# Loading two token tiles by transposing DMA in place of TensorE transposes, with the first loads redistributed over two issuing queues

## The chip, the cores and the metric

One NeuronCore of a Trainium2 chip runs the whole program. The metric is the device time of one execution in microseconds (us). The kernel before took 288.73 us in the median of three runs (288.58 to 288.88). The profile below comes from one further execution of 288.21 us, whose span from first to last instruction is 287.0 us.

## The reference

The input is x, 2048 tokens of 640 values (bf16). Two branches are computed from it and mixed by a gate per token:

```python
x = A_x
g = _sigmoid((x * gate_w).sum(-1, keepdims=True))
a = _A_ref(x, A_wqkv, A_w_phi, A_wo)              # linear attention, 32 heads of 20
b = _B_ref(x, B_w_gate, B_w_up, B_w_down)         # SwiGLU, 1728 hidden columns
return g * a + (1 - g) * b
```

In the attention branch q, k and v are projections of x. q and k go through w_phi (20x20 for each head), and the softmax of the result and of its negative, side by side, are the features. The k features and v are summed over all tokens to a small matrix for each head, the q features multiply it, and the result goes through wo.

## The kernel before, in words

The tokens are cut into 16 tiles of 128 (t0 to t15), and four tiles make a block of 512. TensorE needs x with its 640 columns on the partitions, so each token tile lives in SBUF as `xT[:, t, c, :]`, five 128x128 pieces. There are two ways in which a tile gets there:

- Tiles 0 to 3 are loaded as they lie into `xs` (`load_x`, L369, on the queue that `XQ` at L361 names), transposed on TensorE by five matmuls against the identity into PSUM (`xpose`, L458, recorded at L308), and copied to `xT` by VectorE (recorded at L320).
- Tiles 4 to 15 are read by transposing DMAs on SyncE's queue straight into `xT` (`load_xt`, L372, recorded at L349).

The q and k weights are premultiplied by w_phi on chip: `load_wt` (L391) reads five row blocks of the k weights by transposing DMAs into `wT`, `w_blocks` (step Y, L559) spreads `wph` into `wbd` on VectorE and GpSimd, and `premult` (steps M0 to M4, L565) multiplies them.

Every instruction goes through a small recorder (`_Tracker.run`, L145), which keeps the order of the program for each engine and adds the semaphore waits that the data needs. The order is written out by hand in two lists. `LOADS` (L33) is issued first: x0 is the plain load of tile 0, w0 to w4 are the five row blocks of the v weights (160 KB each, queue by `WQ`, L362), g the gate vector, f0 the first 256 gate and up columns, h is w_phi, k0 to k4 are the `wT` transposing DMAs, t4 to t15 those of the token tiles. SyncE's and ScalarE's issues follow that list, each in its own order. `ORDER` (L38) is the computation: H is warm-up matmuls, X a tile's transposes, `U t.c` the c-th fifth of the v projection of tile t (two matmuls, `vpart`, L499), V a whole v projection (ten matmuls), F0.k the k-th 128 gate and up columns for block 0 (five matmuls on `wg`, five on `wu`), K, S, P, E the steps of the k features.

At the start ORDER is H0 to H12, X0, G, X1, then the v projections of tiles 0, 1 and 2 interleaved by weight row block, with X2 and X3 put between them, then V3, Y, F0.1, M1, M0 and so on.

Two groups of waits on a semaphore value that has long been reached stand in the code: `NPEW` (L20) waits in TensorE's stream in `kv_end` (step N, L749), after the k features are summed, and `NWAIT` (L19) in ScalarE's in `fitem`. They wait for nothing.

`load_phi` (L387) makes ScalarE wait for the landing of w3 before it issues the w_phi load. ScalarE's table load and its first copies out of PSUM stand behind that in its stream.

Of the kernel before, what the change touches and what calls it, by code (L numbers as in the profile page):

```python
# [6 lines left out]
P = 128  # L7
# [9 lines left out]
NV = 6  # L17
NWARM = 2
NWAIT = 6  # L19
NPEW = 24  # L20
FP = 120 * NCH
FK = FP + 8
ACTF = mybir.ActivationFunctionType
# [7 lines left out]


LOADS = """  # L33
x0 w0 x1 g w1 x2 w2 x3 w3 w4 f0 h k0 k1 t4 k2 k3 k4 t5 t6 t7 t8 t9 t10 t11 t12 t13 t14 t15 q0 q1 q2 q3
q4 f1 f2
"""

ORDER = """  # L38
H0 H1 H2 H3 H4 H5 H6 H7 H8 H9 H10 H11 H12 X0 G X1 U0.0 U1.0 U0.1 X2 U1.1 U2.0 U0.2 U1.2 U2.1
X3 U2.2 U0.3 U1.3 U2.3 U0.4 U1.4 U2.4 V3 Y F0.1 M1 i3 M0 F0.0 M2 V4 M3 M4 K0 K1 I S0 V6 V5 S1 P0  # L40
K3 K2 P1 E0 V9 K4 E1 S3 V7 P3 K5 S2 V8 V10 S4 P2 P4 E2 R0 E3 K6 S5 P5 S6 i4 E4 V14 K7 K8 P6 V15 S7
R2 E5 K9 S8 P7 R1 E6 K10 S9 V12 P8 E7 P9 K11 S10 P10 F0.2 R3 F1.2 E8 E9 K12 E10 S11 S12 K14 S14
V11 K13 P11 P12 E11 K15 P14 R4 S13 P13 F1.9 S15 P15 E12 V13 T F1.8 E13 F1.11 E14 Q1 E15 Q0 Q2 N A0
# [10 lines left out]
class _Tracker:  # L54
# [90 lines left out]
    def run(self, eng, fn, reads=(), writes=(), dma=False):  # L145
        rkeys = list(dict.fromkeys(k for a in reads for k in self.keys_of(a)))
        wkeys = list(dict.fromkeys(k for a in writes for k in self.keys_of(a)))
        need = {}

        def req(ev, raw):  # L150
            if ev is None:
                return
            s, v = ev
            if s == eng and not dma and (eng == "pe" or not raw):
                return
            if v > need.get(s, 0):
                need[s] = v

        for k in rkeys:
            for kk in self._conflicts(k):  # L160
                req(self.lastw[kk], True)
                if k[0] == "psum":
                    for s, v in self.readers[kk].items():
                        req((s, v), False)
        for k in wkeys:
            for kk in self._conflicts(k):
                req(self.lastw[kk], True)
                for s, v in self.readers[kk].items():
                    req((s, v), False)
        self._wait(eng, need)  # L170
        ins = fn()
        if dma:
            sn = "d%d" % self.ndma
            self.ndma += 1
            self._add_sem(sn)
            inc = 16
        else:
            sn, inc = eng, 1
        ins.then_inc(self.sem[sn], inc)
        self.cnt[sn] += inc  # L180
        v = self.cnt[sn]
        snap = dict(self.known[eng])
        if not dma:
            snap[sn] = max(snap.get(sn, 0), v)
        self.evknow.setdefault(sn, {})[v] = snap
        ev = (sn, v)
        for k in wkeys:
            self.lastw[k] = ev
            self.readers[k] = {}
        for k in rkeys:  # L190
            r = self.readers[k]
            if r.get(sn, 0) < v:
                r[sn] = v
        return ev


def _build(nc, A_x, A_wqkv, A_w_phi, A_wo, B_x, B_w_gate, B_w_up, B_w_down, gate_w, out):
    tr = _Tracker(nc)
    pe, act, dve, pool, sp = nc.tensor, nc.scalar, nc.vector, nc.gpsimd, nc.sync
# [3 lines left out]
    def sb(name, shape, dtype):  # L203
        t = nc.alloc_sbuf_tensor(name, list(shape), dtype)
        tr.reg(t, "sbuf", nc.lookup_mloc(t).addr)
        return t
# [6 lines left out]
    wg = sb("wg", [P, 5, F_FFN], BF16)  # L213
    wu = sb("wu", [P, 5, F_FFN], BF16)
# [61 lines left out]
    def bank(b, c0, c1, r0=0, r1=P):  # L276
        return ps[r0:r1, b * 512 + c0:b * 512 + c1]
# [38 lines left out]
    def copy(e, o, i):  # L316
        if e == "act":
            return actop(o, i, ACTF.Copy)
        eo = tr.eng[e]
        return run(e, lambda: eo.tensor_copy(o, i), [i], [o])  # L320

    def tt(e, o, a, b, op):
        eo = tr.eng[e]
        return run(e, lambda: eo.tensor_tensor(o, a, b, op), [a, b], [o])  # L324
# [9 lines left out]
    def reduce(o, i):  # L334
        return run("dve", lambda: dve.tensor_reduce(o, i, AX.X, ALU.add), [i], [o])  # L335
# [8 lines left out]
    def dma(e, dst, src, transpose=False):  # L344
        eo = tr.eng[e]

        def fn():
            if transpose:
                return eo.dma_start_transpose(dst, src)  # L349
            return eo.dma_start(dst, src)  # L350
        rd = [src] if src.tensor.name in tr.base else []
        wr = [dst] if dst.tensor.name in tr.base else []
        return run(e, fn, rd, wr, dma=True)
# [5 lines left out]


    XQ = ["sp", "act", "act", "act"]  # L361
    WQ = ["act", "sp", "sp", "sp", "act"]  # L362
    x2 = A_x[0]
    out2 = out[0]

    def load_rows(e, dst, c, c0):
        return dma(e, dst, A_wqkv[c * P:(c + 1) * P, c0:c0 + D])
# [5 lines left out]
        dma("sp", xT[:, t, :, :], x2[t * P:(t + 1) * P, :], transpose=True)  # L373

    def load_ffn(c0, c1):
        dma("sp", wg[:, :, c0:c1], B_w_gate[:, c0:c1].rearrange("(c p) j -> p c j", p=P))
        dma("sp", wu[:, :, c0:c1], B_w_up[:, c0:c1].rearrange("(c p) j -> p c j", p=P))

    wv_evs = []

    def load_wv(c):
        wv_evs.append(load_rows(WQ[c], wvg[:, c, 0:D], c, 2 * D))

# [1 line left out]
        dma("sp", gwr[0:5, :], bass.AP(gate_w.tensor, gate_w.offset, [[P, 5], [1, P]]))  # L385

    def load_phi():  # L387
        tr._wait("act", dict([wv_evs[3]]))
        dma("act", wph[:, :, :], A_w_phi.rearrange("h e f -> (h e) f").rearrange("(c p) f -> p c f", p=P))

    def load_wt(which, m):  # L391
# [9 lines left out]
    H0 = [0, 6, 12, 19, 25]  # L401
    H1 = [7, 13, 20, 26, 32]
# [172 lines left out]
    def kv_finish():  # L575
        for bk, j0, j1 in ((KV0, 0, 8), (KV0 + 1, 8, NCH)):
            n = j1 - j0
            i = bank(bk, 0, 63 * n, 0, 120).rearrange("p (j h d) -> p j h d", h=3, d=DH + 1)
            tt("dve", zt[0:120, j0:j1, :], i[:, :, :, DH],
               hmask[0:120, :].unsqueeze(1).to_broadcast([120, n, 3]), ALU.mult)  # L580
        reduce(zf[0:120, :], zt[0:120, :, :])
        copy("dve", zh[0:120, 0:NCH], zf[0:120, :])
        for bk, j0, j1 in ((KV0, 0, 8), (KV0 + 1, 8, NCH)):
            n = j1 - j0
            i = bank(bk, 0, 63 * n, 0, 120).rearrange("p (j h d) -> p j h d", h=3, d=DH + 1)
            for hh in range(3):
                tt("dve", kvsb[0:120, j0:j1, 20 * hh:20 * hh + 20], i[:, :, hh, 0:DH],
                   hmask[0:120, hh:hh + 1].unsqueeze(1).to_broadcast([120, n, DH]), ALU.mult)
# [160 lines left out]
    def kv_end():  # L749
        for _ in range(NPEW):  # L750
            pe.wait_ge(tr.sem["pe"], 1)
        kv_finish()
        ring["n"] = 4

    ops = {
        "H": lambda i: warm(), "i": fills, "X": xpose, "G": gcol, "U": vpart, "V": vtile,
        "M": lambda m: premult(1, m), "R": lambda m: premult(0, m),
        "K": ktile, "S": knorm, "P": kmul, "p": lambda t: kmul(t, "dve"), "E": kvtile, "x": load_x, "t": load_xt, "w": load_wv, "g": load_gate, "h": load_phi, "k": lambda m: load_wt(1, m), "q": lambda m: load_wt(0, m),
        "f": lambda i: load_ffn(FCUT[i], FCUT[i + 1]), "L": load_late_weights, "T": tail_weights, "J": gates,
        "Y": w_blocks, "I": kv_begin, "N": kv_end, "Z": z_row,  # L760
        "Q": qtile, "A": qsum, "B": qden, "C": qscale, "c": qmul,
        "F": fitem, "O": oitem, "D": ditem,
# [6 lines left out]
def bass_gated_mix__linear_kernel_hedgehog__swiglu_ffn__prompt_kernel(  # L769
    nc: bass.Bass,  # L770
    A_x: bass.AP,
    A_wqkv: bass.AP,
    A_w_phi: bass.AP,
    A_wo: bass.AP,
    B_x: bass.AP,
    B_w_gate: bass.AP,
    B_w_up: bass.AP,
    B_w_down: bass.AP,
    gate_w: bass.AP,
    out: bass.AP,  # L780
):
    _build(nc, A_x, A_wqkv, A_w_phi, A_wo, B_x, B_w_gate, B_w_up, B_w_down, gate_w, out)
# [28 lines left out]
```

The softmax here doesn't subtract the row's maximum and nothing guards it: scores larger than these inputs give would overflow.

## Time and profile before

| what | value | where it is from |
|---|---|---|
| median of three runs | 288.73 us | the times |
| span of the profiled execution | 287.0 us | the page |
| TensorE busy | 284.1 us, 1979 matmuls | the page, part 1 |
| granted TensorE clock | 1.0 | the cores' list |
| matmuls on `xs` (the transposes) | 20, from 3.8 to 7.8 us | the answer on the tile `xs` |
| first matmul of F0.1 | 11.19 us | the timeline |
| hardware queue of SyncE (q1) | 47400 packets, 20.43 MB | the page, part 3 |
| hardware queue of ScalarE (q10) | 1520 packets, 0.87 MB | the page, part 3 |

Times on the timeline count from the start of the span. A row of the timeline gives start, length, engine, source line (that of the recording helper), operation, the tiles written and read, and how many instructions were merged into the row; "SPq" and "ACTq" are DMA issues on SyncE and ScalarE. The landing of a DMA is given as the time from its issue. A matmul's length on the page covers its whole passage through the array; successive ones overlap, and what counts is the distance between their starts.

### The profile page before, as it was taken

The numbers are of one execution on the slowest core, as the hardware profiler recorded it, in microseconds if no ns is written. First come the engines' busy times: TensorE is split into PE (matmuls) and PEld (weight loads), VectorE is DVE, ScalarE is ACT, GpSimd is POOL, SyncE is SP. The second block draws the span as 40 slices with busy tenths as digits, with TensorE's granted clock in tenths as the row PEclk, the third lists the DMA queues.
The fourth block names the chain that finished last, engine by engine and source line by source line (L and its number), as shares of the span: only waits on it lengthen the run. The fifth ranks groups of instructions, "written<-read, shape, count | busy, mean of one in ns | idle before, by whom it ended". The sixth has DMA issues, their size and how long they took to land.

```text
span 287.0 us, 4972 instructions
## 1 busy us (share of the span) xinstructions
PE 284.1 (99%) x1979; PEld 174.5 (61%) x1979; DVE 163.3 (57%) x243; ACT 152.4 (53%) x256; POOL 159.8 (56%) x125
## 2 busy tenths in 40 slices
PE   8999999999999999999999999999999999999997
PEld 6667777575644545557775556675554446666776
DVE  2337748576569978689991465970317899100000
ACT  0767778576775465683535753225676552234112
POOL 8286999879446789836543438350754558501000
PEclk9999999999999999999999999999999999999999
DMA  7977697000010598202383002061020006210101
GB/s 234 192 113 127 113 279 279 3 1 2 0 50 0 123 290 162 50 2 50 66 157 69 6 1 50 2 149 43 2 50 0 3 1 123 53 46 0 49 23 48
DMA packets 48944, 21.62 MB, mean 75 GB/s; under 512 B 39384, under 2 KB 48792, under 8 KB 48920
## 3 DMA queue, kind: packets, MB, share of 16 engines
q1 hardware_dynamic: 47400, 20.43, 31.5%
q10 hardware_dynamic: 1520, 0.87, 1.0%
q8 instruction: 16, 0.26, 0.4%
q14 instruction: 8, 0.07, 0.1%
HBM read 9.29 MB, written 2.62 MB: 42 GB/s over the span
## 4 chain that ended last, share of the span: by engine, by line
PE 99%; DVE 0%; issue 0%
PE ps L296 97%; PE ps L478 1%; PE ps L308 0%; DVE xT L320 0%; DVE osb L737 0%; DVE wvg L320 0%
## 5 line engine op out<-in xcount | busy, mean ns | idle before, releaser
L324 POOL TENSOR_TENSOR hT<-hT,us 128x512 bf16<-128x512 bf16 (+1 forms) x56 | 65.0, 1174 | 65.1 <-DVE hT L328 47.5
L328 DVE SCALAR_TENSOR_TENSOR hT<-hT,ps 128x512 bf16<-128x512 bf16 (+1 forms) x56 | 37.4, 683 | 66.8 <-ACT hT L314 53.0
L296 PE MATMUL ps<-xT,wg 128*128 128x512 bf16 x260 | 64.6, 379 | 0.0
L296 PE MATMUL ps<-xT,wu 128*128 128x512 bf16 x260 | 64.6, 379 | 0.0
L296 PE MATMUL ps<-wd,hT 128*128 128x320 bf16 (+2 forms) x462 | 63.9, 295 | 0.0
L324 POOL TENSOR_TENSOR ph<-eq,qc 128x1320 bf16<-128x1320 bf16 x16 | 42.4, 2647 | 25.6 <-DVE qc L638 20.8
L296 PEld LDWEIGHTS ps<-wd,hT 128*128 128x128 bf16 x462 | 44.5, 98 | 17.5 <-issue 0.2
L296 PE MATMUL ps<-wqk,xT 128*128 128x320 bf16 x320 | 47.7, 299 | 0.0
L314 ACT ACTIVATE hT<-ps 128x512 bf16<-128x512 f32 (+2 forms) x64 | 36.4, 569 | 16.8 <-PE ps L296 16.5
L296 PEld LDWEIGHTS ps<-xT,wu 128*128 128x128 bf16 x260 | 25.5, 98 | 30.6
L314 ACT ACTIVATE us<-ps 128x512 bf16<-128x512 f32 (+1 forms) x56 | 33.5, 598 | 18.5 <-PE ps L296 17.3
L314 ACT ACTIVATE osb<-ps,omg 128x640 bf16<-128x640 f32 (+2 forms) x17 | 12.9, 758 | 55.4 <-PE ps L296 55.4
L296 PEld LDWEIGHTS ps<-xT,wg 128*128 128x128 bf16 x260 | 25.1, 98 | 27.8 <-ACT osb L314 0.8
L324 POOL TENSOR_TENSOR ekr<-ekr,krec 128x1280 bf16<-128x1280 bf16 x16 | 37.4, 2358 | 5.8 <-DVE krec L338 5.8
L296 PEld LDWEIGHTS ps<-wqk,xT 128*128 128x128 bf16 x320 | 30.5, 98 | 13.1 <-issue 0.4
L314 ACT ACTIVATE eq<-ps 128x640 bf16<-128x640 f32 x32 | 22.4, 704 | 20.9 <-POOL ph L324 10.8
L335 DVE TENSOR_REDUCE ksum<-ekr 128x64 f32<-128x1280 bf16 x16 | 23.5, 1471 | 11.7 <-ACT ekr L314 11.7
L314 ACT ACTIVATE ekr<-ps 128x640 bf16<-128x640 f32 x32 | 22.3, 704 | 8.7 <-PE ps L296 8.2
L335 DVE TENSOR_REDUCE qz<-eq 128x64 f32<-128x1280 bf16 x16 | 23.6, 1478 | 2.6 <-ACT eq L314 2.6
L296 PE MATMUL ps<-wog,oT 128*128 128x320 bf16 (+2 forms) x165 | 24.7, 294 | 0.0
L296 PE MATMUL ps<-wvg,xT 128*128 128x320 bf16 (+1 forms) x160 | 24.1, 299 | 0.1
L335 DVE TENSOR_REDUCE qw<-ez 128x64 f32<-128x1280 bf16 x16 | 23.6, 1477 | 0.0
(73 smaller groups left out, 188.6 us busy)
## 6 DMA issues: line engine op xcount, KB each, us to landing
out_dram<-osb SPq DMA_DIRECT2D x15, 160.0 KB, 2.0
wd<-in_B_w_down_dram SPq DMA_DIRECT2D x1, 2080.0 KB, 9.2
wg<-in_B_w_gate_dram SPq DMA_DIRECT2D x1, 1040.0 KB, 10.0
wu<-in_B_w_up_dram SPq DMA_DIRECT2D x1, 1040.0 KB, 12.2
wg<-in_B_w_gate_dram SPq DMA_DIRECT2D x1, 800.0 KB, 6.1
wu<-in_B_w_up_dram SPq DMA_DIRECT2D x1, 800.0 KB, 7.7
wog<-in_A_wo_dram SPq DMA_DIRECT2D x2, 375.0 KB, 7.1
xs<-in_A_x_dram ACTq DMA_DIRECT2D x3, 160.0 KB, 4.2
```

The lines of the kernel that those rows point to most:

```text
L296: last = pe.matmul(o, lhsT=l, rhs=r, start=st, stop=sp_, skip_group_check=sk)
L314: return run("act", lambda: act.activation(o, i, func, scale=scale), rd, [o])
L324: return run(e, lambda: eo.tensor_tensor(o, a, b, op), [a, b], [o])
L328: return run("dve", lambda: dve.scalar_tensor_tensor(out=o, in0=a, scalar=s, in1=b, op0=op0, op1=op1), rd, [o])
L335: return run("dve", lambda: dve.tensor_reduce(o, i, AX.X, ALU.add), [i], [o])
L478: last = pe.matmul(bank(2 * pr, 0, P), lhsT=c, rhs=c, start=True, stop=True)
```

## The change

Tiles 2 and 3 are no longer loaded into `xs` and transposed on TensorE. They come as `t2` and `t3`, transposing DMAs on SyncE's queue, directly behind w1. The v weight rows w2 and w3, the first gate and up columns (f0, two DMAs) go from SyncE's queue to ScalarE's. The w_phi load loses its wait for w3. ORDER loses X2 and X3; the v projections of tiles 0 and 1 stay interleaved by fifths, and that of tile 2 becomes a whole step, V2, ahead of V3. TensorE's group of empty waits at step N grows from 24 to 44, and SyncE gets four at the same place. On TensorE ten matmuls go, on VectorE three copies.

```diff
-NPEW = 24
+NPEW = 44
 LOADS = """
-x0 w0 x1 g w1 x2 w2 x3 w3 w4 f0 h k0 k1 t4 k2 k3 k4 t5 t6 ...
+x0 w0 x1 g w1 t2 t3 w2 w3 w4 f0 h k0 k1 t4 k2 k3 k4 t5 t6 ...
 ORDER = """
-H0 ... H12 X0 G X1 U0.0 U1.0 U0.1 X2 U1.1 U2.0 U0.2 U1.2 U2.1
-X3 U2.2 U0.3 U1.3 U2.3 U0.4 U1.4 U2.4 V3 Y F0.1 M1 i3 M0 F0.0 M2 V4 M3 M4 K0 ...
+H0 ... H12 X0 G X1 U0.0 U1.0 U0.1
+U1.1 U0.2 U1.2 U0.3 U1.3 U0.4 U1.4 V2 V3 Y F0.1 M1 i3 M0 F0.0 M2 V4 M3 M4 K0 ...
-    WQ = ["act", "sp", "sp", "sp", "act"]
+    WQ = ["act", "sp", "act", "act", "act"]
     def load_ffn(c0, c1):
-        dma("sp", wg[:, :, c0:c1], ...)
-        dma("sp", wu[:, :, c0:c1], ...)
+        e = "act" if c0 == 0 else "sp"
+        dma(e, wg[:, :, c0:c1], ...)
+        dma(e, wu[:, :, c0:c1], ...)
     def load_phi():
-        tr._wait("act", dict([wv_evs[3]]))
         dma("act", wph[:, :, :], ...)
     def kv_end():
         for _ in range(NPEW):
             pe.wait_ge(tr.sem["pe"], 1)
+        for _ in range(4):
+            sp.wait_ge(tr.sem["pe"], 1)
```

## The prediction, made before the changed kernel ran

> **What bounds the kernel now.** I read the page's busy shares and its chain by engine first:
>
> ```profile
> PE 284.1 (99%) x1979; PEld 174.5 (61%) x1979; DVE 163.3 (57%) x243; ACT 152.4 (53%) x256; POOL 159.8 (56%) x125
> ...
> PE 99%; DVE 0%; issue 0%
> ```
>
> TensorE is busy for 284.1 of 287.0 us and the chain that ends last runs through it alone. Busy does not mean dense, so next the chain in order of time (start, length, what):
>
> ```profile
> 3.77 0.72 PE ps L308 x5
> 4.50 0.02 issue
> 4.52 0.42 DVE xT L320
> 4.94 0.10 DVE wvg L320
> 5.04 0.05 issue
> 5.09 1.00 PE ps L296 x6
> 6.08 0.32 PE ps L308 x5
> 6.40 1.37 PE ps L296 x10
> 7.78 0.28 PE ps L308 x5
> 8.05 69.40 PE ps L296 x640
> ```
>
> Until 5.09 the chain waits for data and copies. From 5.09 on it is TensorE without a break; the starts in the timeline confirm it (the 24 v matmuls from 7.89 to 11.19 stand 137.5 ns apart). So whatever leaves TensorE's stream after 5.09 comes off the end one for one, and whatever makes it stop is added one for one. The two rows with L308 after 5.09 are X2 and X3. Last, the DMA issues in the timeline, and the answers on the tiles `wT` and `xT` (duration of an issue min/median/max in ns, then time to landing in us):
>
> ```profile
> 2.69 0.45 ACTq L350 DMA_DIRECT2D wvg<-in_A_wqkv_dram  x1
> 3.00 0.43 SPq L350 DMA_DIRECT2D wg<-in_B_w_gate_dram  x1
> 3.48 0.53 SPq L350 DMA_DIRECT2D wu<-in_B_w_up_dram  x1
> 4.05 4.23 SPq L349 DMA_TRANSPOSE wT<-in_A_wqkv_dram  x2
> 7.30 0.40 ACTq L350 DMA_DIRECT2D wph<-in_A_w_phi_dram  x1
> ```
>
> ```profile
> L349 SPq DMA_TRANSPOSE wT<-in_A_wqkv_dram x5: 1277/1299/2820, 4.0 to 12.3; - x5
> DMA to landing us min/median/max: 3.8/4.7/6.2
> ```
>
> ```profile
> L349 SPq DMA_TRANSPOSE xT<-in_A_x_dram x12: 1277/1278/2122, 8.3 to 27.7; - x12
> DMA to landing us min/median/max: 2.9/3.9/4.9
> ```
>
> A transposing DMA holds SyncE for 1.28 us against 0.4 for a plain one. The first of all (L349, at 4.05) held it 2.82.
>
> **What the Trainium skill says.** "TensorE: Matmul & The Clock Gate", section "Wait — 56ns, not 53.3ns?", gives 55.6 ns between warm matmuls of 128 columns; here the transposes of X3 start 56 ns apart, five in 0.28 us. "DMA: Bandwidth & Descriptors", section "Issuing engines are not separate DMA queues", says that SyncE's and ScalarE's DMAs share the same 16 engines. The trace agrees: w1, x2, w2, x3, w3, w4, from both queues, landed at 5.47, 5.91, 6.34, 7.05, 7.29, 7.79, one 160 KB tile in 0.46 us. So moving loads between queues buys no bandwidth, only order and issue time. Section "Queues, rings and completion order" of that page says that a DMA engine takes turns between the queues by packet. Between 5.0 and 5.5 the packet records show 65 packets of SyncE's queue and 67 of ScalarE's, which fits.
>
> **TensorE's part.** Between the first U matmul (5.09) and F0.1 (11.19) lie 6.10 us. The 40 v matmuls there, 30 in U steps and 10 in V3, take 40 x 137.5 ns = 5.50. The remaining 0.60 is X2 (5.95 to 6.24), X3 (7.61 to 7.89) and a 0.03 wait for x2. After the change 20 matmuls are U steps and 20 are V2 and V3: the same 40. Best case **-0.60 us**. VectorE's three copies (0.65 and 0.49 us of its time) hide under TensorE; nothing waits for VectorE there afterwards, so they count nothing.
>
> **The deadlines this sets.** With TensorE never stopping, the data is needed at: w2 after 8 matmuls, 6.19; w3 6.74; w4 7.29; t2 7.84; t3 9.21; wg 10.59; wu 11.67; M1 (wT1 and `wbd`) 12.75, which was 13.35.
>
> **The supply.** *ScalarE's queue.* w2 takes the slot of x2 (issued 1.73, landed 5.91), in time. w3 and w4 come in the slots at 2.21 and 2.69, whose loads landed at 7.05 and 7.79. But two plain tiles have left SyncE's queue ahead of them, 2 x 0.46, replaced by transposed packets that cannot start until their issue is over (3.4) and w1's are out (4.60). I take w3 6.2, w4 6.8; both bounds (6.1 to 7.0, 6.4 to 7.6) reach at most 0.3 past the deadline. wg and wu are issued 0.2 later than before and landed at 8.72 and 9.75; there is 1.9 us to spare.
> *t2.* Issued at 2.06. Lower bound: the median 3.9 gives 6.0. A transposed tile has 640 packets of 256 B (18 ns each on one of 16 engines) against 55 ns for the 1280 B packets of a weight row and 27 for those of wg. Taking turns from 4.60 on, 40 turns per engine, some 18 with rows (73 ns) and 22 with wg (45 ns), end at 6.9; w1 landed 0.87 after its last packet, so 7.8. With the 2.82 us issue: 8.5. Deadline 7.84.
> *t3.* Issued at 3.4. Lower bound 7.3. Forty turns with wg behind t2: 8.7, landed 9.6. With the long first issue 10.4. Deadline 9.21.
> Which value I take: for w_phi, issued on ScalarE at 7.30 while SyncE generated transposes, the first packet came 2.8 us later (x0: 1.0). If wg is held likewise it starts at 6.0, not 5.0, and t2 lands near 7.2, t3 near 9.0. The 2.82 I put down to wg and wu queued ahead (1280 small packets): the wu issue at 38.08, behind three such loads, also took 1.24 in place of 0.5. That queue is empty at 2.06. So I take both **in time, 0**.
> *The later transposes.* t2 and t3 (2 x 1.32 with the gap between issues) stand where w2, w3, wg, wu took 1.99 (2.06 to 4.05), so wT0 and all behind move by +0.65, or by -0.9 if the 1.54 extra goes with wg and wu. wT4 has 1.1 to spare (landed 17.04, used 18.14), t6 1.35, later tiles more. With -0.60 for TensorE at worst 0.15 late; I take 0.
> *w_phi.* Issued at 4.2 instead of 7.30, but behind wg and wu. Y needs 1.58 from landing (11.38) to the last `wbd` (12.96), so it must land by 11.2. Bounds: 8.3 (its 4.1 from issue) and 11.6 (after wu at 10.5, its 640 packets in turns with transposes 1.2). Taken 10.5: 0; at worst +0.4. ScalarE's table load was free to run at 7.79 and is now at 5 to 7, ahead of the first copy (9.46); nothing behind it is delayed.
>
> **The empty waits.** In TensorE's records 24 of them are 11 instructions, 109 ns apart, from 74.87 to 75.96. The wait for VectorE that follows was over at 76.16, and the next matmul started at 77.29: the array had 17 matmuls in stock. Ten more instructions are 1.09 us and bring that wait to about 77.15, the matmul to 77.25 to 77.4. Cost 0 to 0.1; taken **+0.03**. Behind them stands the whole remaining stream. SyncE's one more wait instruction falls between 39.3 and 79.1, where it issues nothing: 0.
>
> **Sum.** 287.0 - 0.60 + 0.03 = 286.43 of span. The median run (288.73) lies 1.73 above this span, so **288.2 us**.
>
> **Rivals.**
> 1. *Late by a little.* The queues take strict turns, t3 lands at 9.4 to 10.3 and V3 waits: F0.1 starts at t3 + 1.42, 10.8 to 11.7 against 11.19. For: the packet counts above. Against: w_phi's long start. 288.4 to 289.2, middle 288.8.
> 2. *Slower.* The first transposing DMA costs 2.82 by itself, wherever it stands; t2 lands at 8.5, t3 at 10.4, F0.1 starts at 11.8, 0.6 later than before: 289.4. It decides as soon as t3 lands after 9.77. With `wbd` late as well, up to 290. For: the 2.82 is on record and is the first. Against: the backlog explains it too, and a queue backlog is seen again at 38.08.
> 3. *The empty waits eat the gain.* If the stock of matmuls were smaller by ten then they would cost up to 0.6: 288.7. Against: the 17 counted.
>
> **Chances.** In time 0.50 (own range 288.0 to 288.4), rival 1 with rival 3 0.20, rival 2 0.30. A measurement here can tell about 0.2%, 0.58 us: the full gain is just that, so I split the first case in halves: faster 0.25, same 0.25 + 0.20 = 0.45, slower 0.30. Range 288.0 to 289.9: it leaves out the worst of rival 2 and the best of case one, under 2 in 10.
>
> **What would show it.** Right: no L308 rows after 5.09; v matmuls 137.5 ns apart from 5.09 on; F0.1 at 10.59; t2 landed before 7.84, t3 before 9.21, its issue 1.3 us; the matmul after step N without a gap. Wrong: TensorE idle before V2, V3 or M1 with a DMA or `wbd` as what ended it, a first issue of 2.8, a hole of tenths after the waits at step N. A move of over 0.7 us either way with F0.1 at 10.6 would mean that something after the start counts that I have taken as rigid.

## The result and the profile after

The changed kernel took **290.14 us** in the median of four runs (289.86 to 290.28), the kernel before, now in four runs, 288.81 (288.58 to 289.17). The ratio is 1.0044 with a 95% interval of 1.0026 to 1.0061: slower by 0.4%, and above the range of the prediction. The profiled execution was one of 289.86 us with a span of 288.6, against 288.21 and 287.0 before: +1.6.

The page of the changed kernel, first its busy times, then its chain by engine:

```profile
PE 284.3 (99%) x1969; PEld 174.5 (60%) x1969; DVE 162.3 (56%) x240; ACT 152.6 (53%) x256; POOL 159.8 (55%) x125
...
PE 95%; DMA 3%; SPq 1%; issue 0%; DVE 0%
```

TensorE has its ten matmuls less, and its share of the chain has gone from 99% to 95%: a DMA has come in. The chain in order of time (start, length, what) names it:

```profile
2.07 1.32 SPq L349
3.39 0.05 issue
3.43 7.98 DMA xT<-in_A_x_dram
11.41 0.05 issue
11.46 67.65 PE ps L296 x626
```

One transposing DMA, t3, issued at 3.43, lands 7.98 us later at 11.41. TensorE starts again at 11.46. In the timeline of the same kernel (the bracket gives the idle time ahead of a row and what ended it):

```profile
4.91 5.00 PE L296 MATMUL ps<-wvg,xT 128*128 128x320 bf16 x30
...
11.46 1.55 PE L296 MATMUL ps<-wvg,xT 128*128 128x320 bf16 x10 [1.54 <-DMA xT<-in_A_x_dram]
...
12.84 1.24 PE L296 MATMUL ps<-xT,wg 128*128 128x512 bf16 x5
```

The 30 matmuls of U and V2 run through; V3 stands 1.54 us for t3; F0.1 starts at 12.84 in place of 11.19. That is +1.65, the whole difference of the spans: from F0.1 to the end it is 275.8 us in both kernels. Behind F0.1 there is no other loss. The answer on the tile `xT` (issue in ns min/median/max, then landing in us) shows how far t3 lies off:

```profile
L349 SPq DMA_TRANSPOSE xT<-in_A_x_dram x14: 1272/1278/2552, 2.1 to 29.1; - x14
DMA to landing us min/median/max: 2.9/3.3/8.0
```

The rest of what was to be watched: the first transposing issue took 1.32, t2 landed at 7.58, w2, w3 and w4 at 5.67, 6.28 and 7.22, wg, wu and w_phi at 9.18, 11.30 and 11.93. At step N, the last matmuls ahead of the empty waits and the first one behind them, before:

```profile
74.58 2.88 PE L296 MATMUL ps<-wqk,xT 128*128 128x320 bf16 x20
...
77.29 0.22 PE L308 MATMUL ps<-ident,zh 120*128 120x120 bf16 x1
```

and after:

```profile
76.23 2.88 PE L296 MATMUL ps<-wqk,xT 128*128 128x320 bf16 x20
...
78.94 0.22 PE L308 MATMUL ps<-ident,zh 120*128 120x120 bf16 x1
```

2.71 us from start to start in both: twenty more waits cost nothing.

What the 16 DMA engines did meanwhile is in the table by stage (each row a stretch in us, its length, the busy shares and counts of the five engines, the granted clock, the DMA share, and last the GB/s). Before:

```profile
5.00:6.00 1.00, 0.91 (x7) 0.56 (x8) 0.47 (x3) 0.00 (x0) 0.94 (x2) 1.00 1.03 358
6.00:7.00 1.00, 1.00 (x12) 0.72 (x12) 0.65 (x2) 0.00 (x0) 1.00 (x3) 1.00 1.08 363
7.00:8.00 1.00, 1.00 (x12) 0.79 (x11) 0.00 (x0) 0.21 (x1) 0.17 (x1) 1.00 1.16 335
8.00:9.00 1.00, 1.00 (x10) 0.69 (x8) 0.49 (x1) 1.00 (x1) 0.00 (x0) 1.00 1.59 268
```

After:

```profile
5.00:6.00 1.00, 1.00 (x6) 0.52 (x6) 0.42 (x1) 0.97 (x1) 0.94 (x2) 1.00 1.17 224
6.00:7.00 1.00, 1.00 (x7) 0.66 (x6) 0.00 (x0) 0.31 (x1) 1.00 (x3) 1.00 1.18 242
7.00:8.00 1.00, 1.00 (x10) 0.71 (x8) 0.00 (x0) 0.00 (x0) 0.16 (x1) 1.00 1.16 257
8.00:9.00 1.00, 1.00 (x9) 0.73 (x8) 0.00 (x0) 0.69 (x3) 0.00 (x0) 1.00 1.26 239
```

The DMA share adds up packet times that overlap, so it passes 1; it is much the same in both. But in these four us the engines bring 962 KB instead of 1324 (the sums of the last column). The packet records have longer packets in the mean: 1280 B took 55 to 58 ns before (5 to 7 us) and 95 between 5 and 6 us after; 512 B took 27 or 28 before (6 to 8 us) and 37 to 52 after (6 to 10 us). The typical packet is as it was: the median of the 1280 B ones stays at 55, and 24 of the 137, of up to 614 ns, make the mean. (Fewer bytes and dearer 1280 B packets turn up again below in kernels where t3 is in time, so they don't set the changed kernel apart.) The records also show a stop. t2 and t3 have 640 packets of 256 B each. The 640th started at 6.88, the next only at 7.60; from 7 to 8 us 17 packets of 256 B and 494 of ScalarE's 512 B packets started.

### The profile page after: what moved, and what is told of

Read it like the earlier page. It is cut to its first block, busy times and chain, and to the rows that moved or that the text cites. A ratio compares the mean times of both kernels' runs of the same rounds, so it can differ in the third digit from the quotient of the medians.

```text
span 288.6 us, 4961 instructions
## 1 busy us (share of the span) xinstructions
PE 284.3 (99%) x1969; PEld 174.5 (60%) x1969; DVE 162.3 (56%) x240; ACT 152.6 (53%) x256; POOL 159.8 (55%) x125
## 3 DMA queue, kind: packets, MB, share of 16 engines
HBM read 8.97 MB, written 2.62 MB: 40 GB/s over the span
## 4 chain that ended last, share of the span: by engine, by line
PE 95%; DMA 3%; SPq 1%; issue 0%; DVE 0%
PE ps L296 95%; DMA xT<-in_A_x_dram 3%; SPq L349 0%; SPq L350 0%; DVE osb L737 0%; PE ps L308 0%
## 5 line engine op out<-in xcount | busy, mean ns | idle before, releaser
L296 PE MATMUL ps<-wvg,xT 128*128 128x320 bf16 (+1 forms) x160 | 24.7, 305 | 1.5 <-DMA xT<-in_A_x_dram 1.5
```

The lines of the kernel that those rows point to most:

```text
L296: last = pe.matmul(o, lhsT=l, rhs=r, start=st, stop=sp_, skip_group_check=sk)
```

## The experiments

My theory after these lines: **t3 is late because gate and up columns (f0) on ScalarE's queue run beside the transposed packets on SyncE's.** Rivals: the early transposing DMAs are slow whatever lies beside them; the empty waits; the moves of the loads between queues cost something even without t2 and t3; it is the amount of data ahead of t3. One table first. "F0.1" is the start of its first matmul; for the rest see the text. Times in us, the profile's left, the runs' right. Each ratio is to runs of the kernel before from the same round: 25 to 42 of them for the experiments, with medians of 288.59 to 288.65.

| label | base and edit | t3 landed | F0.1 | span | median (runs) | ratio to before, 95% |
|---|---|---|---|---|---|---|
| before, after | | –, 11.41 | 11.19, 12.84 | 287.0, 288.6 | 288.81, 290.14 | 1.0044 [1.0026, 1.0061] |
| e1_f0_sp | after, f0 on SyncE behind t3 | 8.83 | 10.94 | 287.2 | 288.45 (20) | 0.9993 [0.9983, 1.0003] |
| e2_pad24 | after, waits as before | 12.29 | 13.73 | 289.5 | 290.7 (4) | 1.0063 [1.0038, 1.0088] |
| e3_queues_only | before, loads moved | – | 11.46 | 288.3 | 290.19 (15) | 1.0046 [1.0032, 1.0061] |
| e4_f0_sp_phi | e1, w_phi waits for w4 | 8.05 | 10.73 | 287.4 | 288.59 (12) | 1.0004 [0.9994, 1.0013] |
| e5_f0_after_t3 | after, f0 only when t3 is there | 8.78 | 12.98 | 289.8 | 292.48 (4) | 1.0131 [1.0103, 1.0158] |
| e6_t3_only | t2 as before, t3 by DMA, f0 on SyncE | 8.50 | 11.65 | 287.4 | 288.82 (14) | 1.0010 [0.9999, 1.0022] |
| e7_changed_again | after, once more | 11.29 | 12.73 | 288.5 | 289.95 (4) | 1.0055 [1.0035, 1.0075] |
| e8_before_pad44 | before, waits of after | – | 12.81 | 288.6 | 288.36 (12) | 0.9994 [0.9983, 1.0005] |
| e9_wu_sp | after, only wu on SyncE | 11.10 | 12.54 | 288.5 | 289.54 (18) | 1.0032 [1.0022, 1.0042] |
| e10_f0_sp_f02 | e1, F0.2 ahead of M3 and M4 | 9.47 | 11.75 | 287.6 | 288.89 (14) | 1.0005 [0.9993, 1.0017] |
| e11_f0_act_only | before, f0 on ScalarE, nothing else | – | 11.74 | 288.9 | 290.18 (5) | 1.0071 [1.0045, 1.0097] |
| e12_one_queue | e1, w2 to w4 and w_phi on SyncE too | 8.90 | 10.95 | 287.2 | 289.6 (6) | 1.0047 [1.0034, 1.0061] |
| e13_one_queue_f02 | e12, F0.2 ahead of M3 and M4 | 8.97 | 10.88 | 286.7 | 288.29 (21) | 0.9991 [0.9982, 1.0000] |

### f0 back on SyncE's queue

```diff
     def load_ffn(c0, c1):
-        e = "act" if c0 == 0 else "sp"
+        e = "sp"
```

> The changed kernel with one part undone: the first gate and up columns are issued on SyncE again, behind t3. Sharing theory (t3 is late because wg, wu and w_phi from ScalarE's queue take turns with it and the two kinds of packets slow each other): t3 lands at 8.0 to 9.4, F0.1 starts at 10.6 to 11.2 instead of 12.84, time 288.2 to 289.0. Rival (a transposing DMA this early is slow whatever runs beside it): t3 lands at 11 or later as in the changed kernel, time 290.0 to 290.3. A third way: t3 is early but wg or wT1, now behind one another on one queue, come late and TensorE stops before F0.1 or M1; then 288.8 to 290 with that wait in the trace.

t2 and t3 landed at 7.90 and 8.83 and V2 and V3 didn't wait. The landings of all transposing DMAs into `xT`, where the changed kernel has one of 8.0:

```profile
DMA to landing us min/median/max: 2.9/3.5/5.8
```

The first matmuls of F0.1 and of M4 in the timeline:

```profile
10.94 1.24 PE L296 MATMUL ps<-xT,wg 128*128 128x512 bf16 x5
...
18.37 0.49 PE L296 MATMUL ps<-wbd,wT 128*128 128x140 bf16 x6 [0.31 <-DMA wT<-in_A_wqkv_dram]
```

F0.1 comes 0.25 earlier than before, though this execution ran its V matmuls at the slow distance until 5.6 us (last section), which cost about 0.3. Then M4 waits for wT4, which landed at 18.32 (17.04 before): ahead of the wT transposes in SyncE's queue there are now t2 and t3 as well as f0, where the kernel before had w2, w3 and f0, and wT4 is issued at 13.61 instead of 12.29. So the loss of the change is gone, and its gain in this execution is paid at M4, which starts about 0.5 late.

The stage table of this kernel says what is not the cause:

```profile
5.00:6.00 1.00, 1.00 (x8) 0.61 (x6) 0.56 (x3) 0.98 (x1) 0.94 (x2) 1.00 1.12 248
6.00:7.00 1.00, 1.00 (x9) 0.68 (x7) 0.00 (x0) 0.30 (x1) 1.00 (x3) 1.00 1.38 181
7.00:8.00 1.00, 1.00 (x9) 0.59 (x7) 0.00 (x0) 0.00 (x0) 0.16 (x1) 1.00 1.34 135
8.00:9.00 1.00, 1.00 (x9) 0.70 (x8) 0.43 (x2) 0.89 (x3) 0.38 (x1) 1.00 1.20 254
```

These four us bring 818 KB, less than the 962 of the changed kernel, and the mean 1280 B packet took 82 ns between 5 and 6 us; yet t3 is in time. What differs is whose packets run: from 7 to 8 us 459 transposed ones started here, 17 in the changed kernel. Nor is it any packet of ScalarE's queue: between 6 and 7 us 601 of w_phi's 40 B packets started beside 541 transposed ones, without a stop.

### The empty waits, from both sides

```diff
-NPEW = 44
+NPEW = 24
     def kv_end():
...
-        for _ in range(4):
-            sp.wait_ge(tr.sem["pe"], 1)
```

> The changed kernel with the empty waits as before (24 on TensorE, none on SyncE). If they cost what the forecast took, 0 to 0.1 us less: 290.0 to 290.2. If the empty waits carry a part of the loss, 0.5 us or more less than the changed kernel, and its trace shows the matmul after step N without the gap that the changed one then has.

Without the added waits the kernel stays slow. In the timeline the two waits of TensorE:

```profile
8.67 2.10 PE L296 MATMUL ps<-wvg,xT 128*128 128x320 bf16 x14 [0.87 <-DMA wvg<-in_A_wqkv_dram]
12.34 1.55 PE L296 MATMUL ps<-wvg,xT 128*128 128x320 bf16 x10 [1.57 <-DMA xT<-in_A_x_dram]
```

Here w4 was late as well (landed 8.62). The other side is the kernel before with the waits of the changed one:

```diff
-NPEW = 24
+NPEW = 44
     def kv_end():
...
+        for _ in range(4):
+            sp.wait_ge(tr.sem["pe"], 1)
```

> The kernel before with the changed kernel's empty waits (44 on TensorE, four on SyncE) and nothing else: the forecast's 0 to 0.1 us more, so within 0.2 us of before, and no gap ahead of the transposes after step N. If the stock of matmuls is too small to cover them, up to 0.6 more and a gap there.

Its ratio of 0.9994 holds 1. The profiled execution happened to be a long one (289.87 us, its median is 288.36), with w2 landed at 8.36 instead of 6.34 and 1.07 us of waiting for it, and again no gap at step N. So the empty waits are not the loss.

### The moves of the loads, without t2 and t3

```diff
-x0 w0 x1 g w1 x2 w2 x3 w3 w4 f0 ...
+x0 w0 x1 g w1 x2 x3 w2 w3 w4 f0 ...
-    XQ = ["sp", "act", "act", "act"]
-    WQ = ["act", "sp", "sp", "sp", "act"]
+    XQ = ["sp", "act", "sp", "sp"]
+    WQ = ["act", "sp", "act", "act", "act"]
     def load_ffn(c0, c1):
+        e = "act" if c0 == 0 else "sp"
...
     def load_phi():
-        tr._wait("act", dict([wv_evs[3]]))
```

> The kernel before with the queue moves alone: x2 and x3 as plain loads in the places of t2 and t3 on SyncE, transposed on TensorE as before, w2, w3, the first gate and up columns and w_phi on ScalarE as in the changed kernel. Sharing theory with transposed packets as the culprit: everything lands in time, F0.1 at 11.1 to 11.4, 288.6 to 289.1. Rival (the move of w2, w3, f0 and w_phi to ScalarE's queue is itself the loss): wg or wu land after 10.6 and F0.1 starts past 12, 289.5 or more.

This surprised me: with TensorE's transposes back, and so with nothing early about `xT`, the kernel was as slow as the changed one. What is late is another tile; the timeline has it:

```profile
14.69 0.79 PE L296 MATMUL ps<-wbd,wT 128*128 128x140 bf16 x12 [0.91 <-POOL wbd L324]
```

M1 waits for `wbd`, that for w_phi, and w_phi, issued at 4.50, landed at 13.03. So I cut the edit to a single one:

```diff
     def load_ffn(c0, c1):
-        dma("sp", wg[:, :, c0:c1], ...)
-        dma("sp", wu[:, :, c0:c1], ...)
+        e = "act" if c0 == 0 else "sp"
+        dma(e, wg[:, :, c0:c1], ...)
+        dma(e, wu[:, :, c0:c1], ...)
```

> The kernel before with one edit: the first gate and up columns go to ScalarE's queue; tiles 2 and 3 by TensorE, w2 and w3 on SyncE, w_phi waiting for w3 as before. Sharing theory: the columns now run beside the wT transposing DMAs that SyncE issues from 3.0 on; wu and, behind it, w_phi land later than 9.75 and 11.38, wbd comes late, M1 waits 0.5 to 2: 289.2 to 290.6. Rival (the tiles t2 and t3 are needed for the loss): within 0.3 of before.

Its chain in order of time:

```profile
7.47 6.11 DMA wph<-in_A_w_phi_dram
13.58 0.07 issue
13.65 1.50 POOL wbd L324 x3
15.15 0.09 issue
15.24 64.11 PE ps L296 x606
```

w_phi takes 6.11 us from its issue, against 4.1 before: it stands behind wg and wu in ScalarE's queue, and those are late themselves (9.79 and 11.76, before 8.72 and 9.75) beside the wT transposes, which in the kernel before stood behind f0 in one queue. M1 starts 1.34 late behind F0.1, and F0.1 itself 0.55 later than before (11.74), which is the slow start of the last section. **Moving f0 to ScalarE's queue is enough for a loss of this size, without t2 and t3**, though by another tile than in the changed kernel.

### Less of it, later, or only for one tile

Half of f0 moved back:

```diff
     def load_ffn(c0, c1):
...
         dma(e, wg[:, :, c0:c1], ...)
-        dma(e, wu[:, :, c0:c1], ...)
+        dma("sp", wu[:, :, c0:c1], ...)
```

> Half a dose: the changed kernel with only the up columns back on SyncE behind t3, the gate columns still on ScalarE's queue beside t2 and t3. Sharing theory: fewer packets run beside t3 (640 of wg and w_phi's instead of wg's, wu's and w_phi's 1920), so t3 lands between the 8.8 with all of the columns on SyncE and the 11.3 to 11.4 of the changed kernel: 9.2 to 10.4; time 288.4 to 289.6. If t3 lands past 11 as with the full dose, it is not the amount that runs beside it but that something does at all, at the start of t3.

```profile
8.58 2.10 PE L296 MATMUL ps<-wvg,xT 128*128 128x320 bf16 x14 [1.12 <-DMA wvg<-in_A_wqkv_dram]
11.15 1.55 PE L296 MATMUL ps<-wvg,xT 128*128 128x320 bf16 x10 [0.47 <-DMA xT<-in_A_x_dram]
```

A miss in the landing: half the bytes beside t3, and t3 still landed at 11.10. In this profile the amount makes no difference. But w4 was late too (8.53), it is one execution, and the median of 18 runs, 289.54, lies between those of e1 and of the changed kernel, so the amount is not ruled out. The whole of f0 later:

```diff
-... w2 w3 w4 f0 h k0 ...
+... w2 w3 w4 h f0 k0 ...
     def load_ffn(c0, c1):
         e = "act" if c0 == 0 else "sp"
+        if e == "act":
+            run("act", lambda: act.activation(us[:, 2, 0:1], one[:, 0:1], ACTF.Copy), ...)
+            tr._wait("act", dict([xt_evs[3]]))
```

The small activation brings ScalarE's table load ahead of the wait.

> The changed kernel with the gate and up columns still on ScalarE's queue, but issued only when t3 has landed (w_phi goes ahead of them, and a one-column copy ahead of the wait brings ScalarE's table load forward). Nothing runs beside t3 but w_phi. Sharing theory: t3 lands at 8 to 9.2 as with the columns on SyncE (8.8), V3 starts by 9.3; wg is issued at about 9 and lands at 11 to 12, so F0.1 then waits for wg and not for t3: time 288.6 to 289.6. Rival (the queue on which the columns are issued, not the time at which they move): t3 still lands after 10.5, time 290 or more.

```profile
12.98 1.25 PE L296 MATMUL ps<-xT,wg 128*128 128x512 bf16 x5 [1.50 <-DMA wg<-in_B_w_gate_dram]
15.10 1.25 PE L296 MATMUL ps<-xT,wu 128*128 128x512 bf16 x5 [0.86 <-DMA wu<-in_B_w_up_dram]
```

With f0 held back t3 lands at 8.78: the late tile follows f0, in this direction too. But wg, issued only at 8.80, landed 4.1 us later and wu, beside the wT transposes, at 15.05, and the kernel is the slowest of all. In e6_t3_only tile 2 went back to TensorE (x2, X2 and its U steps as before), with f0 on SyncE:

```diff
-x0 w0 x1 g w1 t2 t3 w2 w3 w4 ...
+x0 w0 x1 g w1 t3 x2 w2 w3 w4 ...
-NPEW = 44
+NPEW = 34
```

> Half of the idea: tile 2 as a plain load on ScalarE's queue with its TensorE transposes, tile 3 alone by a transposing DMA behind w1, gate and up columns on SyncE, w2, w3, w_phi on ScalarE. TensorE's stream is 0.28 shorter than before and SyncE's queue 1.3 shorter than with both tiles. Sharing theory: t3 lands by 8.3, V3 is not held, wT4 lands before M4 needs it, 288.2 to 288.5 against 288.6 to 288.8 of before. Rival (any transposing DMA among the first loads costs more than it saves): 288.8 or more, with TensorE waiting for a weight row, t3 or wT4.

t3 at 8.50 and no wait for any DMA; the V matmuls ran at the slow distance until 6.8 us, which cost about 0.8 us in this execution. The median, 288.82, is above the 288.2 to 288.5 expected and no better than before; one profile doesn't tell why the 14 runs gain nothing. The changed kernel once more, for the size of its own scatter:

> The changed kernel once more, beside the others on one chip: 289.9 to 290.5. In its profile V3 waits for t3 again, landed between 10.5 and 12.5. If the landing of t3 differs by a microsecond from the first profile, the spread from execution to execution is of the transfers.

t3 at 11.29, V3 waiting 1.83 us: with e2 there are three profiled executions of t3 beside the whole of f0 on the other queue, 11.29 to 12.29.

### What is left when t3 is in time

With f0 on SyncE (e1) the w_phi load lies beside t3. Holding it until w4 is there:

```diff
     def load_phi():
+        tr._wait("act", dict([wv_evs[4]]))
```

> As the run with the gate and up columns back on SyncE, and ScalarE waits for the landing of w4 before it issues w_phi, so that its 640 small packets stay away from t2 and t3. Sharing theory: t3 lands 0 to 0.8 earlier than without that wait, F0.1 at 10.6 to 10.9; the risk is wbd: w_phi lands at about 11.2 and M1 waits up to 0.4. 288.2 to 288.8. Rival: no difference to the run without the wait in t3's landing.

t3 came still earlier (8.05), but w_phi landed at 12.09 and M1 started 0.86 late: one wait for another. Against the wait at M4, columns 256 to 384 of block 0 were put ahead of M3 and M4 in e10:

```diff
-... k0 k1 t4 k2 k3 k4 ...     f1 f2
+... k0 k1 t4 k2 f1 k3 k4 ...  f2 f3
-... F0.0 M2 V4 M3 M4 ...      P10 F0.2 R3 ...
+... F0.0 M2 V4 F0.2 M3 M4 ... P10 R3 ...
-    FCUT = [0, 256, 896, F_FFN]
+    FCUT = [0, 256, 384, 896, F_FFN]
```

> The kernel with both tiles by transposing DMA and the gate and up columns on SyncE, whose trace lost 0.47 us to wT4 at M4, with one gate and up step more (F0.2, 2.16 us of work taken from later, its columns loaded between k2 and k3) ahead of M3 and M4. If that wait is what keeps it from the full gain: no wait at M4, 287.9 to 288.3 against 288.6 of before. If not, 288.4 to 288.8: the columns make wT3, wT4 and the tiles behind them late by as much as the step gives.

The M4 wait was gone, but in the profiled execution w4 landed at 8.39 and TensorE waited 0.96 for it: a miss, and no gain.

Two readings were open by then: plain packets of one queue beside transposed packets of the other, or the early transposing DMAs themselves. e12 leaves only one queue in play:

```diff
-x0 w0 x1 g w1 t2 t3 w2 w3 w4 f0 h ...
+x0 w0 x1 g w1 w2 w3 w4 t2 t3 h f0 ...
-    WQ = ["act", "sp", "act", "act", "act"]
+    WQ = ["act", "sp", "sp", "sp", "sp"]
     def load_phi():
-        dma("act", wph[:, :, :], ...)
+        dma("sp", wph[:, :, :], ...)
```

(on top of f0 on SyncE).

> SyncE's queue alone carries, from the second tile of wv on, wv rows 2, 3, 4, then x2 and x3 transposed, then w_phi, wg, wu and the rest; ScalarE's has only wv row 0 and x1. No plain packet of another queue lies beside a transposed one any more, but x2 and x3 still arrive by two early transposing DMAs. Sharing theory (transposed packets of one queue beside plain packets of the other are what is slow): w4 lands by 7.3, t2 by 8.0, t3 by 9.0, no wait ahead of V2 and V3, F0.1 at 10.6 to 11.2; the transposes of w_o that follow in the same queue come later by up to 1 us, so M4 may wait 0.4 to 1.1 for wT4: 288.0 to 288.9. Rival (the early transposing DMA is slow by itself, whatever lies beside it): t3 at 9.7 or later, w_phi and wg behind it late too, F0.1 at 11.5 or later, 289.5 to 291.

(What this text calls the transposes of w_o are the wT transposes, of the k weights.)

The two transposing DMAs issued at 3.49 and 4.85 landed at 7.80 and 8.90, w4 at 6.79. The landings of all transposing DMAs into `xT` (us):

```profile
DMA to landing us min/median/max: 3.0/4.0/5.0
```

None takes over 5.0, where the changed kernel has one of 8.0. So **the early transposing DMAs are not slow by themselves**. (Its 1280 B packets took 98 ns in the mean between 4 and 5 us, with one queue only, and it brought 814 KB between 5 and 9 us: again neither figure goes with a late t3.) But the runs are slow: 289.6 in the median, which is in the rival's range and outside the 288.0 to 288.9 of the sharing theory; it is the landings that decide between the two. The chain of the profiled execution, the shortest of the six runs, has the place:

```profile
14.47 3.67 DMA wT<-in_A_wqkv_dram
18.14 0.05 issue
18.19 59.50 PE ps L296 x562
```

The fifth wT transpose comes last, and M4 waits 0.29 for it. That is no more than in e1 (0.31), so it doesn't explain why the other runs of e12 are slower than those of e1. e13 adds the edit of e10 to that:

> The kernel of one queue, and the gate and up work of columns 256 to 384 put ahead of M3 and M4 on TensorE (it is there in the kernel before at another place; the amount of work is unchanged), so that M4 has 1.3 us more until it needs wT4. Sharing theory: the same landings as with one queue, M4 waits 0 to 0.2, 287.8 to 288.4. Rival as there: t3 at 9.7 or later, 289.3 to 291, since work put ahead of M4 doesn't help V3.

```profile
7.93 2.93 PE L296 MATMUL ps<-wvg,xT 128*128 128x320 bf16 x20 [0.19 <-DMA xT<-in_A_x_dram]
...
10.88 1.25 PE L296 MATMUL ps<-xT,wg 128*128 128x512 bf16 x5
```

A wait of 0.19 for t2 is what is left; M4 doesn't wait, and the span is 286.7. The median fell from 289.6 to 288.29 through the edit of e10 alone, so the rest of e12's loss probably lay at M4; how long it waited there in the longer executions no profile shows. Against the kernel before, e13 is ahead by 0.3 us in the median, with an interval that just reaches 1: better than the changed kernel without doubt, better than the one before perhaps. Whether the kernel before would gain as much from F0.2 ahead of M3 and M4 was not tried.

## Why the prediction was wrong

**The failed step is the supply of t3: "I take both in time, 0".** In its own terms it should have been +2.2: t3 landed at 11.41, 2.2 behind the deadline of 9.21, and 286.43 + 2.2 is the 288.6 of the span. TensorE stood idle for 1.54 of that; the other 0.7 went into V matmuls that still ran at the slow distance, so that TensorE came to V3 at 9.92 and not at 9.21. The prediction worked out 9.6 for t3 with packets by turns and then took 9.0. Part by part:

- *The price of a packet.* 18, 27 and 55 ns are right for the typical packet, in the changed kernel too. They leave out the few that take hundreds of ns, which bring the means to 95 and to 37 to 52. But e1 and e12, with means of 82 and 98 for 1280 B, have t3 in time, so this alone didn't make it late.
- *Turns by packet.* This is the part that failed. From 7 to 8 us, where equal turns would be about as many of each, 17 transposed packets stood against 494. (The 65 and 67 that spoke for equal turns were plain 1280 B packets on both sides.) A stop after the 640th, so behind a whole tile, is in every kernel profiled with f0 on ScalarE's queue while transposes run from SyncE's: 0.72 us here, 0.77 (e7), 0.41 (e2), 0.96 (e9), 1.00 (e3), 1.26 (e11), and in e5, where f0 comes later, 1.22 behind the fifth tile. With f0 on SyncE and t3 directly behind t2 (e1, e4, e10, e12, e13) the 641st follows without one. The section "Queues, rings and completion order" of the Trainium skill's "DMA: Bandwidth & Descriptors" calls a packet some 9 to 17 descriptors, with 64 at most; I had read the records in the trace as such packets. If they are single descriptors, 640 on 16 engines are 40 on each, and a whole tile may go in a turn or a few. That fits the stop; no run here shows which engine a packet ran on, so it is a reading.
- *From the last packet to the landing.* Taken 0.87, from w1. Counted through, t3's last 256 B packet started at 9.36 (worked out 8.7): 2.05 ahead of its landing. In e1 and e12 it is 0.9. Half of the 2.05 is packets again: behind its 640 each transposed tile has 32 of 4 B in the same queue, and those of t3 started from 8.95 to 10.40 (t2's from 6.46 to 6.90, t3's in e1 from 7.91 to 7.99). From the last of them to the landing it is 1.01, against 0.85 in e1. So of the 1.8 us by which the worked-out 9.6 fell short, about 0.7 is the tile's 256 B packets, 1.0 the 4 B ones behind them and 0.1 the rest.

The choice of the better value rested on w_phi's late first packet. f0's first packet came indeed late, at 6.47, and it did not help.

**A second gap stands in a sentence of the prediction:** that moving loads between queues "buys no bandwidth, only order and issue time". Order can also be lost, and it costs: e11 pays 1.6 us in the median for the move of f0 alone, since w_phi now stands behind wu, and since the wT transposes no longer stand behind f0, so that wg and wu themselves come 1.1 and 2.0 later. Whether rate was lost besides isn't shown: e11 brought 1130 KB between 5 and 9 us against 1324, but has transposed packets of 256 B in that stretch from 6 us on, the kernel before only from 8 on. The case that the queue moves lose by themselves was not among the rivals.

Point by point for the rest:

- *TensorE's part, -0.60.* Right, as far as it can be seen: the L308 rows after 5.09 are gone, and where t2 and t3 are in time F0.1 starts at 10.73 to 10.95 (e1, e4, e12, e13) although some of these executions ran slow V matmuls. The whole gain didn't follow: e13, with M4 fed as well, gains 0.3 us in the median and not 0.57. That its 288.29 stands near the predicted 288.2 is partly luck, since the kernel before stood at 288.62 in that round and not at 288.73.
- *The first transposing issue.* 1.32, as taken, so the mechanism of rival 2 (2.82 by itself) fell. The backlog reading is not settled by it: in e12 wT0's issue took 1.22 behind w_phi, wg and wu. The rival's deciding point, "as soon as t3 lands after 9.77", was right, and so was its sign, for another reason; t3 came later than its 10.4, so the time came out above its 289.4.
- *t2.* Worked out 7.8 by turns, taken 7.2, landed 7.58, in time for 7.84 (7.90 in e1, 7.80 in e12: the margin is thin).
- *w2, w3, w4.* Taken w3 6.2 and w4 6.8; 6.28 and 7.22, inside the bounds.
- *w_phi.* Taken 10.5, landed 11.93, outside the bounds. In the changed kernel the wait for t3 hid it; the last `wbd` was there at 13.50, which is 0.75 behind the 12.75 at which M1 would have needed it with t3 in time (an estimate from these two figures).
- *The later transposes.* wT4 landed at 18.04, 1.0 later than before, where at most 0.65 was allowed; hidden as well, since V3 had pushed M4 back. In e1 and e12, where V3 is in time, it is the next wait.
- *The empty waits.* +0.03 taken, 0.00 measured (2.71 us across step N in both).
- *The offset of 1.73 from span to median.* A run's time stands 1.2 to 1.3 over its own span in both kernels (288.21 and 287.0, 289.86 and 288.6). The other 0.5 is real: the profile of before was a short execution (288.21, where the median is 288.7). Its early end of the slow start, in the last section, fits that.

What stays open: what makes the transposed queue stop behind a tile when f0 is in the other queue, why the 4 B packets of t3 then come so late, and why half of f0 did as much as the whole. That f0 on ScalarE's queue beside t3 makes t3 late is shown by e1 and e5 against the changed kernel and e7; how the turns bring it about is not.

## What to carry to other kernels

Before moving a load to another queue "because the DMA engines are shared anyway", look at what the other queue carries at that moment: the price of a packet doesn't tell whose turn it is, and a tile with a deadline belongs in the order of one queue, not in a race between two. A tile that just misses its deadline hides later ones behind its wait; mend it, and the next (here wT4 at M4) takes its place, so check all deadlines of the stage against the same supply. And a gain of 0.2% at the start of a kernel is worth less than the spread of the landings that it comes to rely on.

## What the runs showed of the hardware

- **TensorE's slow start ends at a different moment in each execution.** The distance of the v matmuls changes from 270 to 138 ns (that of the transposes from 107 to 56) at 4.5 us in the profile of before, at 6.5 in that of after, where the wait for t3 hid it, and between 3.9 (e5) and 6.8 (e6) in the others; at the late end six matmuls at 270 instead of 138 cost 0.8 us. The Trainium skill's "TensorE: Matmul & The Clock Gate", section "What's actually happening", gives a free-running window as the reason and 500 ns either way; these profiles lie 2.9 us apart. A median of several runs is needed for any comparison below 0.3%.
- **A single plain 160 KB load now and then lands 1 to 2 us late**, with no cause in the queues that I could find: w2 at 8.36 in e8 (6.34 before), w4 at 8.39 to 8.62 in e2, e9 and e10 (7.22 after). A landing is the last of 16 semaphore updates, and only one or two of them were late: for w2 in e8 15 had come by 6.71.
- **The issue of a transposing DMA is not of one length.** It is 1.2 to 1.3 us at the shortest and longer in some executions, mostly where many small packets are waiting: wT0's took 2.82 before, 1.50 after, 2.36 in e1, 3.79 in e9 and 4.93 in e8, but 1.22 in e12, behind w_phi, wg and wu, so waiting packets alone don't settle it.
